# Hyena gate behind an RWKV-6 recurrence: a full inverse transform, sums from PSUM, interleaved products, and the key copy on VectorE

## The chip, the cores and the metric

The kernel runs on one core of one Trainium2 chip. The metric is the device time of one execution in microseconds (us), as the median of several runs. A "profiled span" is the length of the one execution that the profiler recorded; it is some 2 us shorter than the timed runs. Runs are marked fast or slow by their time (slow: over 1.5% above the fastest run of the same kernel); the comparisons of times below use the fast ones. The "granted clock" is the share of TensorE's full clock that the profiler shows it was given; 0.5 is half clock.

The program keeps its tiles in two memories: SBUF, and PSUM, to which it has TensorE write the results of all its matmuls and transposes.

## The reference, cut to what matters

Two stages stand one after the other. Stage 1 is a linear-attention recurrence over 768 steps for 4 batches and 8 heads of 48 columns. Stage 2 takes its output as `x` (4 x 768 x 384), projects it three ways, convolves one part with a filter through a real Fourier transform, gates it with the other two, and projects it out.

```python
# stage 1, per step t
cur = np.einsum('bhd,bhe->bhde', u[None] * kt, vt)
y[:, :, t] = np.einsum('bhd,bhde->bhe', rt, state + cur)
state = wt[:, :, :, None] * state + np.einsum('bhd,bhe->bhde', kt, vt)
# stage 2
x1, x2, x3 = split(x @ w_proj, 3)
X2 = np.fft.rfft(x2, n=S, axis=1)
H  = np.fft.rfft(filter_fft, n=S, axis=0)[None]
x2_conv = np.fft.irfft(X2 * H, n=S, axis=1)
return ((x1 * x2_conv * x3) @ w_out).astype(np.float32)
```

## The kernel before

Stage 1 works on chunks of 128 steps, six to a batch, 24 in all. One chunk is a serial loop across the engines:

- GpSimd scales the keys (`kh`), TensorE transposes them into PSUM (`tk`), and an engine copies them to SBUF (`tkT`).
- TensorE makes the scores (`sc`), VectorE masks them (`mt`), TensorE makes the output (`yn`), ScalarE copies it (`xn`), TensorE transposes it (`yt`), and ScalarE copies that into the tile `xT` for stage 2.

The start of `mt` is the clock by which I measure chunks: "chunk 9 at 81.0" means that its masked scores started 81.0 us into the span.

Stage 2 is cut into pieces that wait in a list, `pending`. Three calls of `fill` per chunk take pieces from it, by a budget of units. A unit is a group of matmuls plus its way out of PSUM. In the timelines of these runs VectorE and ScalarE run their operations in the order in which the program emits them, also where the first has to wait and the second could go (in chunk 0 of after the keys lie ready at 12.63, and the key copy on VectorE starts at 14.59, behind a bonus sum that waits 1.68 us for GpSimd; the key copy back on ScalarE, below, shows such a place too: ready at 81.46, started at 82.67). So the place of a call in the program is its place in its engine's queue.

```python
    def turn(idx):                       # start of a chunk
        tk = psA.tile([L, HP, L], BF16, tag="a", name="tk")
        ...                              # four transposes of kh
        nc.scalar.activation(out=tkT, in_=tk, func=AF.Copy)

    def turn_x(idx, xT):                 # end of a chunk
        yt = psA.tile([L, CB, L], BF16, tag="a", name="yt")
        ...                              # three transposes of xn
        nc.scalar.activation(out=xT[:, :, ci * L:(ci + 1) * L], in_=yt, func=AF.Copy)
    # ---- stage 2 of a batch (cut) ----
        def sums(ti):                    # once each for chunks 3, 4, 5 of a batch
            lo = xT[:, :, ti * L:(ti + 1) * L]
            hi = xT[:, :, HALF + ti * L:HALF + (ti + 1) * L]
            nc.vector.tensor_add(z("sd0")[:, :, sl], lo, hi)
            nc.vector.tensor_sub(z("sd1")[:, :, sl], lo, hi)

        def prods(sl):                   # six operations in a row, 128 x 1152 each
            nc.vector.tensor_mul(ua, xr, HR[:, sl, :])
            ...                          # mul, sub, mul, mul, add

        def inv(cb):                     # even and odd halves by symmetry, then combined
            ...                          # four full and four half-row matmuls -> ev, od
            nc.scalar.activation(out=ods, in_=od, func=AF.Copy)
            nc.vector.tensor_add(eo[:, 0, :], ev, ods)
            nc.vector.tensor_sub(eo[:, 1, :], ev, ods)
            nc.vector.tensor_mul(z("y")[:, cb, :], eo.rearrange("p q t -> p (q t)"), z("g")[:, cb, :])
        ...
            ready[5] += fws + [F(prods, slice(0, 3))]
            ready[5] += g1[0:4] + invs[0:1] + g1[4:6] + invs[1:3]
    # ---- the loop over chunks (cut) ----
    FILL = (2, 2, 2, 0)
            turn(idx); begin(idx + 2); load_weights(idx); issue_loads(idx + 4); fill(FILL[0])
            ...                          # late pieces join pending here
            scores(idx); decay(idx + 1); bonus_b(idx + 1); bonus_a(idx + 2); fill(FILL[1])
            output(idx); fill(FILL[2])
            turn_x(idx, xTs[b])
            ...                          # sums of this chunk, at once
                if idx == 3:
                    late = filters + late      # transform of the filter, six units
```

In the profile's names, `sd` are the sums, `X` the spectra, `U` and `P` the products, `g` the gate, `cc` the bonus sum of stage 1, `lw` the logarithm of the decay.

Of the kernel before, what the change touches and what calls it, by code (L numbers as in the profile page):

```python
# [10 lines left out]
FP32 = mybir.dt.float32  # L11
BF16 = mybir.dt.bfloat16
INT32 = mybir.dt.int32
AF = mybir.ActivationFunctionType
ALU = mybir.AluOpType
# [5 lines left out]
L = 128  # L21
NCH = S // L
C = H * D
CB = C // L
HP = H // 2
DP = 64
HALF = S // 2
NT = HALF // L
# [6 lines left out]
def kernel(  # L35
# [12 lines left out]
    nc = tc.nc  # L48
# [121 lines left out]
    nc.vector.memset(blk[DP:L, 1:2], 1.0)  # L170

    scl0 = consts.tile([L, 1], FP32)
    nc.vector.memset(scl0, 2.0 / S)
    nc.vector.memset(scl0[0:1, :], 1.0 / S)

# [8 lines left out]
    wout = consts.tile([L, CB, C], BF16)  # L184

    def load_weights(n):
        if n == 1:
            nc.sync.dma_start(
                out=filt, in_=moe_filter_fft.rearrange("(n p) c -> p n c", p=L)
            )  # L190
        elif n == -1:
            nc.gpsimd.dma_start(
                out=wproj, in_=moe_w_proj.rearrange("(n p) f -> p n f", p=L)
            )
        elif n == 2:
            nc.gpsimd.dma_start(
                out=wout, in_=moe_w_out.rearrange("(n p) f -> p n f", p=L)
            )

    m2 = consts.tile([L, 6, HALF], BF16)  # L200
    HR = consts.tile([L, 3, C], BF16)
    HI = consts.tile([L, 3, C], BF16)
    HG = consts.tile([L, 3, C], BF16)
# [2 lines left out]
    def ps2(name):  # L206
        return psA.tile([L, C], FP32, tag="a", name=name)
# [28 lines left out]
    sums = {}  # L236

    def setup_m2(q):
        tp = psA.tile([L, NT, L], BF16, tag="a", name="m2t")
        for ti in range(NT):  # L240
            nc.tensor.transpose(tp[:, ti, :], F[:, ti, q * L:(q + 1) * L], ident)
        nc.scalar.activation(out=m2[:, q, :], in_=tp.rearrange("p a b -> p (a b)"), func=AF.Copy)

    def setup_h(q):
        if not sums:
# [73 lines left out]
    def turn(idx):  # L319
        t = st[idx]  # L320
        kh = k_bufs[idx % NK]
        tk = psA.tile([L, HP, L], BF16, tag="a", name="tk")
        for j in range(HP):
            nc.tensor.transpose(tk[:, j, :], kh[:, 2 * j:2 * j + 2, :], ident)  # L324
        tkT = s1.tile([L, HP, L], BF16, tag="tkT", name="tkT")
        nc.scalar.activation(out=tkT, in_=tk, func=AF.Copy)  # L326
        t["tkT"] = tkT

    def scores(idx):
# [46 lines left out]
        nc.scalar.activation(out=xn, in_=y, func=AF.Copy)  # L376
        t["xn"] = xn

    def turn_x(idx, xT):
        b, ci = chunks[idx]  # L380
        t = st.pop(idx)
        yt = psA.tile([L, CB, L], BF16, tag="a", name="yt")
        for cb in range(CB):
            nc.tensor.transpose(yt[:, cb, :], t["xn"][:, cb * L:(cb + 1) * L], ident)  # L384
        nc.scalar.activation(
            out=xT[:, :, ci * L:(ci + 1) * L], in_=yt, func=AF.Copy
        )
        if ci < NCH - 1:
            st[idx + 1]["S"] = t["nxt"]
# [3 lines left out]
    stage2 = {}  # L393

    def make_stage2(b, xT):
# [3 lines left out]
            X0=([L, 3, C], BF16, 1), X1=([L, 3, C], BF16, 1),  # L399
            P0=([L, 3, C], BF16, 1), P1=([L, 3, C], BF16, 1),  # L400
            U0=([L, 3, C], BF16, 1), U1=([L, 3, C], BF16, 1),
            sd0=([L, CB, HALF], BF16, 1), sd1=([L, CB, HALF], BF16, 1),
        )
        made = {}

        def z(name):
            if name not in made:
                shape, dt, bufs = shapes[name]
                made[name] = s2.tile(shape, dt, tag=name, name=name, bufs=bufs)
            return made[name]  # L410
# [17 lines left out]
                z("g")[:, fb, sl], proj(2 * C + fb * L, sl), z("x1")[:, fb, sl]  # L428
            )

        def sums(ti):
            lo = xT[:, :, ti * L:(ti + 1) * L]
            hi = xT[:, :, HALF + ti * L:HALF + (ti + 1) * L]
            sl = slice(ti * L, (ti + 1) * L)
            nc.vector.tensor_add(z(f"sd{0}")[:, :, sl], lo, hi)
            nc.vector.tensor_sub(z(f"sd{1}")[:, :, sl], lo, hi)

        def x2(q, ti):
            ps = ps2("ps_x2")
# [8 lines left out]
            ps = fwd(q, z("ab")[:, 0], z("ab")[:, 1])  # L448
            nc.scalar.activation(out=z(f"X{q % 2}")[:, q // 2, :], in_=ps, func=AF.Copy)

        def prods(sl):
            xr, xi, pr, pi, ua, ub = (
                z(n)[:, sl, :] for n in ("X0", "X1", "P0", "P1", "U0", "U1")
            )
            nc.vector.tensor_mul(ua, xr, HR[:, sl, :])
            nc.vector.tensor_mul(ub, xi, HI[:, sl, :])
            nc.vector.tensor_sub(pr, ua, ub)
            nc.vector.tensor_mul(ua, xr, HI[:, sl, :])
            nc.vector.tensor_mul(ub, xi, HG[:, sl, :])
            nc.vector.tensor_add(pi, ua, ub)  # L460

        def inv(cb):
            col = slice(cb * L, (cb + 1) * L)
            ev, od = ps2("ps_e"), ps2("ps_o")
            full = ((0, 0, 0, ev), (1, 1, 0, ev), (4, 0, 2, od), (5, 1, 2, od))
            for n, (q, ri, sl, ps) in enumerate(full):
                nc.tensor.matmul(
                    ps, z(f"P{ri}")[:, sl, col], m2[:, q, :],
                    start=(n % 2 == 0), stop=False,
                )  # L470
            for ri in (0, 1):
                for q, ps in ((0, ev), (1, od)):
                    rows = slice(DP * q, DP * q + DP)
                    nc.tensor.matmul(  # L474
                        ps, z(f"P{ri}")[rows, 1, col], m2[rows, 2 + ri, :],
                        start=False, stop=(ri == 1),
                    )
            ods = s2.tile([L, HALF], FP32, tag="ods", name="ods", bufs=2)
            eo = s2.tile([L, 2, HALF], BF16, tag="eo", name="eo", bufs=2)
            nc.scalar.activation(out=ods, in_=od, func=AF.Copy)  # L480
            nc.vector.tensor_add(eo[:, 0, :], ev, ods)  # L481
            nc.vector.tensor_sub(eo[:, 1, :], ev, ods)  # L482
            nc.vector.tensor_mul(  # L483
                z("y")[:, cb, :], eo.rearrange("p q t -> p (q t)"), z("g")[:, cb, :]
            )

        def outp(ti):
            ps = ps2("ps_o")
# [11 lines left out]
        def F(f, *a):  # L500
            return (COST[f], lambda: f(*a))

        COST = {x1: 1, x3: 1, sums: 0, x2: 1, fw: 1, prods: 0, inv: 2, outp: 1}

        def gates(hf):
            return [F(f, fb, halves[hf]) for fb in range(CB) for f in (x1, x3)]

        ready = {2: gates(0)}
        for ti in range(NT):
            ready[NT + ti] = [F(sums, ti)] + [F(x2, q, ti) for q in (0, 1)]  # L510
        g1 = gates(1)
        fws = [F(fw, q) for q in range(6)]
        invs = [F(inv, cb) for cb in range(CB)]
        if b < B - 1:
            ready[5] += fws + [F(prods, slice(0, 3))]
            ready[5] += g1[0:4] + invs[0:1] + g1[4:6] + invs[1:3]
        else:
            ready[5][1:1] = g1[0:2]
            ready[5] += fws[0:2] + g1[2:3]
            ready[5] += [F(prods, slice(0, 1))] + fws[2:4] + g1[3:4]  # L520
            ready[5] += [F(prods, slice(1, 2))] + fws[4:6]
            ready[5] += [F(prods, slice(2, 3))] + g1[4:6] + invs
        ready[6] = [F(outp, ti) for ti in range(NCH)]
        return ready


# [10 lines left out]
        credit[0] = min(credit[0], 0)  # L537

    xTs = {}
    FILL = (2, 2, 2, 0)  # L540
    issue_loads(2)
    issue_loads(3)
    ENG = mybir.EngineType
    with tc.manual_schedule(engines={ENG.PE, ENG.Activation, ENG.DVE, ENG.Pool, ENG.SP}):
        begin(0)
        decay(0)
        bonus_a(0)
        begin(1)
        bonus_b(0)
        load_weights(-1)  # L550
        bonus_a(1)
        late, outs = [], []
        for idx in range(len(chunks)):
            b, ci = chunks[idx]
            if ci == 0:
                xTs[b] = s2.tile([L, CB, S], BF16, tag="xT", bufs=2, name=f"xT{b}")
            turn(idx)
            begin(idx + 2)
            load_weights(idx)
            issue_loads(idx + 4)  # L560
            fill(FILL[0])
            if late and ci == 3 and outs:
                pending.extend(late)
                pending.extend(outs)
                outs = []
            else:
                pending.extend(late)
            scores(idx)
            decay(idx + 1)
            bonus_b(idx + 1)  # L570
            bonus_a(idx + 2)
            fill(FILL[1])
            output(idx)
            fill(FILL[2])
            turn_x(idx, xTs[b])
            late = []
            if ci == 2:
                stage2[b] = make_stage2(b, xTs[b])
            if b in stage2:
                late = stage2[b].get(ci, [])  # L580
                if ci > 2:
                    late.pop(0)[1]()
                if idx == 3:
                    late = filters + late
                if ci == 5:
                    outs = stage2[b][6]
            fill(FILL[3])
        pending.extend(late + outs)
        fill(1000)
# [30 lines left out]
```

## Time and profile before

| | before |
|---|---|
| median time (runs) | 203.55 us (202.64 to 204.12) |
| profiled span, mean granted TensorE clock | 202.9 us, 0.932 |
| TensorE / VectorE / ScalarE busy | 77% / 76% / 62% |

From the page of before: busy time by engine, the granted TensorE clock in 40 slices of the span (9 is full), and the chain of waits by engine.

```profile
PE 156.5 (77%) x1490; PEld 97.7 (48%) x1490; DVE 153.6 (76%) x249; ACT 126.5 (62%) x269; POOL 121.6 (60%) x162
...
PEclk9999696996999969999999799999997999999678
...
DVE 31%; PE 25%; issue 12%; ACT 12%; DMA 8%; SPq 6%; POOL 4%; DVEq 0%; ACTq 0%; POOLq 0%
```

No engine is full on average. TensorE and VectorE are equally busy, and the chain changes engines all the time. This is a kernel whose regimes alternate, and the next view shows the two: windows of before, with stretch, length, then the busy us of TensorE, its weight loads, VectorE, ScalarE and GpSimd (number of instructions in brackets), granted clock, DMA share and GB/s.

```profile
65.00:73.00 8.00, 4.81 (x45) 2.84 (x43) 7.90 (x9) 3.67 (x8) 7.09 (x6) 0.98 0.56 103
73.00:81.00 8.00, 8.00 (x75) 4.54 (x73) 7.93 (x13) 4.45 (x10) 4.72 (x6) 0.81 0.55 96
...
98.00:103.00 5.00, 5.00 (x59) 3.36 (x57) 3.09 (x5) 4.97 (x13) 3.69 (x6) 1.00 1.18 242
```

In the first two stretches VectorE is full (7.90 and 7.93 of 8 us). In the third it has 2 us to spare and TensorE and ScalarE are full. The VectorE timeline shows what fills the first stretch: start, duration, engine, line, operation, output and inputs.

```profile
65.66 1.39 DVE L456 TENSOR_TENSOR U_1078<-X_962,HI 128x1152 bf16<-128x1152 bf16 x1
...
70.93 1.43 DVE L460 TENSOR_TENSOR P_1076<-U_1077,U_1078 128x1152 bf16<-128x1152 bf16 x1
...
73.22 1.21 DVE L343 TENSOR_TENSOR mt<-sc,mask_excl 128x1024 bf16<-128x1024 f32 x1
```

Six products stand in a row, over 7 us, with stage 1's mask behind them. From chunk 9 on the pattern repeats with a period of 40.8 us: chunk 9 starts at 81.0, chunk 15 at 121.8, chunk 21 at 162.7.

Three waits: engine and line waited for, us in total, times, longest.

```profile
ACT lw_82 L268 <- DMA ld_w<-in_w_dram: 5.2, 1, 5.2
...
PE ps_f L223 <- DVE fs L232: 3.7, 1, 3.7
...
PE ps_e L467 <- DVE P_1076 L460: 3.2, 1, 3.2
```

The first is the load of chunk 5, issued behind the 1152 KB filter load (at 26.8 and 26.1 us): it took 9.4 us from issue to landing, the median of such loads 4.0. The second is TensorE waiting for the sums of the filter. The third is TensorE waiting for the products, once per batch.

Last, the costs of the operations that the change touches, from the groups of instructions: busy us, mean ns of one, then idle time before it.

```profile
L326 ACT ACTIVATE tkT<-tk 128x512 bf16<-128x512 bf16 x24 | 14.4, 598 | 2.1 <-PE tk L324 2.1
...
L483 DVE TENSOR_TENSOR y<-eo,g 128x768 bf16<-128x768 bf16 x12 | 14.0, 1164 | 0.4
```

And the same for the sums, with shapes kept apart:

```profile
L436 DVE TENSOR_TENSOR sd_1353<-xT_866 128x384 bf16<-128x384 bf16 x3 | 2.9, 962 | 0.0
```

`y` takes 1.28 to 1.41 us while GpSimd works and 0.56 us in the tail where it does not. The sums behave alike: 0.35 us at best, 1.16 us at worst. Both read two SBUF inputs.

### The profile page before, as it was taken

The numbers are of one execution on the slowest core, as the hardware profiler recorded it, in microseconds if no ns is written. First come the engines' busy times: TensorE is split into PE (matmuls) and PEld (weight loads), VectorE is DVE, ScalarE is ACT, GpSimd is POOL, SyncE is SP. The second block draws the span as 40 slices with busy tenths as digits, with TensorE's granted clock in tenths as the row PEclk, the third lists the DMA queues.
The fourth block names the chain that finished last, engine by engine and source line by source line (L and its number), as shares of the span: only waits on it lengthen the run. The fifth ranks groups of instructions, "written<-read, shape, count | busy, mean of one in ns | idle before, by whom it ended". The sixth has DMA issues, their size and how long they took to land.

```text
span 202.9 us, 4168 instructions
## 1 busy us (share of the span) xinstructions
PE 156.5 (77%) x1490; PEld 97.7 (48%) x1490; DVE 153.6 (76%) x249; ACT 126.5 (62%) x269; POOL 121.6 (60%) x162
## 2 busy tenths in 40 slices
PE   0177768629989679779996697799976977996962
PEld 0055645416666436546664365466642554653230
DVE  8344553598687999997869999978699999459730
ACT  3866461825989517659996166599961654983242
POOL 5089895577479929459789394597893845100000
PEclk9999696996999969999999799999997999999678
DMA  6999989799987871833989928339930000140024
GB/s 132 198 196 186 207 229 247 152 179 218 189 156 136 156 129 26 155 72 81 288 149 207 176 48 155 60 76 296 168 68 0 5 0 0 57 179 2 0 78 155
DMA packets 104804, 26.41 MB, mean 130 GB/s; under 512 B 100048, under 2 KB 104400, under 8 KB 104784
## 3 DMA queue, kind: packets, MB, share of 16 engines
q1 hardware_dynamic: 103984, 24.98, 60.7%
q0 software_dynamic: 800, 1.18, 3.4%
q8 instruction: 11, 0.18, 0.4%
q14 instruction: 9, 0.07, 0.1%
HBM read 22.61 MB, written 4.72 MB: 135 GB/s over the span
## 4 chain that ended last, share of the span: by engine, by line
DVE 31%; PE 25%; issue 12%; ACT 12%; DMA 8%; SPq 6%; POOL 4%; DVEq 0%; ACTq 0%; POOLq 0%
DMA ld_w<-in_w_dram 8%; DVE mt L343 6%; PE ps_p L415 4%; PE ps_o L490 4%; DVE g L427 4%; ACT tkT L326 3%; PE yn L371 2%; DVE cc L290 2%; SPq L91 2%; ACT ab L445 2%; PE sc L338 2%; DVE eo L481 2%; DVE eo L482 2%; DVE qT L316 2%; ACT o L494 2%
## 5 line engine op out<-in xcount | busy, mean ns | idle before, releaser
L291 POOL TENSOR_TENSOR vc<-v,cc 128x384 bf16<-128x384 bf16 x24 | 21.9, 912 | 34.6 <-PE yt L384 16.5
L343 DVE TENSOR_TENSOR mt<-sc,mask_excl 128x1024 bf16<-128x1024 f32 x24 | 29.2, 1215 | 12.4 <-PE sc L338 12.4
L281 POOL TENSOR_TENSOR rku<-rk,u_bc 128x384 bf16<-128x384 bf16 x24 | 24.4, 1019 | 1.9
L376 ACT ACTIVATE xn<-yn 128x384 bf16<-128x384 f32 x24 | 11.8, 490 | 14.5 <-PE yn L371 13.8
L312 POOL TENSOR_TENSOR kh_83<-ld_k,en 128x384 bf16<-128x384 f32 x12 | 12.0, 1000 | 14.4 <-ACT en L310 14.2
L480 ACT ACTIVATE ods<-ps_o 128x384 f32<-128x384 f32 x12 | 5.9, 490 | 22.8 <-PE ps_o L474 20.6
L415 PEld LDWEIGHTS <-wproj 128*128 128x128 bf16 x144 | 13.9, 104 | 9.1 <-issue 3.5
L310 ACT ACTIVATE en<-csi 128x384 f32<-128x384 f32 x24 | 11.9, 497 | 8.7 <-PE csi L301 7.4
L490 PE MATMUL ps_o<-wout,y 128*128 128x384 bf16 x72 | 15.4, 356 | 1.7 <-DVE y L483 1.6
L326 ACT ACTIVATE tkT<-tk 128x512 bf16<-128x512 bf16 x24 | 14.4, 598 | 2.1 <-PE tk L324 2.1
L316 DVE TENSOR_TENSOR qT<-rT,e_85 128x512 bf16<-128x512 f32 x12 | 8.2, 687 | 9.8 <-PE rT L307 5.3
L290 DVE TENSOR_REDUCE cc<-rku 128x8 f32<-128x384 bf16 x24 | 13.0, 541 | 2.9 <-POOL rku L281 2.9
L282 POOL CAST v<-ld_v 128x384 bf16<-128x384 f32 x24 | 14.4, 602 | 0.0
L483 DVE TENSOR_TENSOR y<-eo,g 128x768 bf16<-128x768 bf16 x12 | 14.0, 1164 | 0.4
L494 ACT ACTIVATE o<-ps_o 128x384 f32<-128x384 f32 x24 | 11.5, 498 | 4.1 <-PE ps_o L490 4.1
L312 POOL TENSOR_TENSOR kh_84<-ld_k,en 128x384 bf16<-128x384 f32 x12 | 13.8, 1148 | 0.2
L371 PE MATMUL yn<-v,mt 128*128 128x48 bf16 x192 | 9.7, 192 | 5.1 <-DVE mt L343 5.1
L338 PE MATMUL sc<-qT,tkT 48*128 48x128 bf16 x192 | 9.7, 222 | 3.8 <-ACT tkT L326 3.3
L301 PE MATMUL csi<-lw_81,mask_incl 128*128 128x384 bf16 x12 | 4.5, 374 | 9.6 <-ACT lw_81 L268 9.6
L363 PE MATMUL yn<-vc,ident 128*128 128x384 bf16 x24 | 9.0, 376 | 3.2 <-ACT en L310 1.8
L371 PEld LDWEIGHTS <-mt 128*128 128x128 bf16 x192 | 7.9, 103 | 6.8 <-DVE mt L343 6.3
L338 PEld LDWEIGHTS <-tkT 48*128 48x128 bf16 x192 | 5.7, 95 | 10.8 <-ACT tkT L326 10.3
(279 smaller groups left out, 482.1 us busy)
## 6 DMA issues: line engine op xcount, KB each, us to landing
ld_w<-in_w_dram SPq DMA_DIRECT2D x24, 192.0 KB, 3.9
ld_k<-in_k_dram SPq DMA_DIRECT2D x24, 192.0 KB, 3.8
ld_v<-in_v_dram SPq DMA_DIRECT2D x24, 192.0 KB, 4.0
out_dram<-o SPq DMA_DIRECT2D x3, 1152.0 KB, 5.1
filt<-in_moe_filter_fft_dram SPq DMA_DIRECT2D x1, 1152.0 KB, 7.8
out_dram<-o SPq DMA_DIRECT2D x6, 192.0 KB, 1.9
r_76<-in_r_dram SPq DMA_DIRECT2D x5, 192.0 KB, 3.6
r_77<-in_r_dram SPq DMA_DIRECT2D x5, 192.0 KB, 4.5
```

What stands on the lines that cost most here:

```text
L281: nc.gpsimd.tensor_mul(t["rku"], rk, u_bc)
L282: nc.gpsimd.tensor_copy(out=t["vb"], in_=t["lv"])
L290: nc.vector.tensor_reduce(out=cc, in_=t["rku"], axis=AX.X, op=ALU.add)
L291: nc.gpsimd.tensor_mul(t["vc"], t["vb"], cc.to_broadcast([L, H, D]))
L312: nc.gpsimd.tensor_mul(kh[:, :, 0:D], t["lk"], en)
L326: nc.scalar.activation(out=tkT, in_=tk, func=AF.Copy)
L338: nc.tensor.matmul(sc[:, par, j, :], tkT[p0:p0 + D, j, :], qT[p0:p0 + D, j, :], start=True, stop=True,)
L343: nc.vector.tensor_mul(mt, sc.rearrange("p q j t -> p (q j) t"), _mid(mask_excl, H))
L371: nc.tensor.matmul(y[:, h, :], mt[:, HP * (h % 2) + h // 2, :], vb[:, h, :], start=False, stop=(h == H - 1),)
L415: nc.tensor.matmul(ps, wproj[:, cb, col0:col0 + L], xT[:, cb, sl], start=(cb == 0), stop=(cb == CB - 1),)
L490: nc.tensor.matmul(ps, z("y")[:, cb, ti * L:(ti + 1) * L], wout[:, cb, :], start=(cb == 0), stop=(cb == CB - 1),)
L494: nc.scalar.activation(out=z("o")[:, ti, :], in_=ps, func=AF.Copy)
```

## The change

Its intent is to take work off VectorE and ScalarE and give it to TensorE.

- **Inverse.** It computes all 768 rows with matmuls (twelve per column block, with negated copies `m2n` of the transform). There is nothing to copy out and combine: `y` is one multiply per half, straight from PSUM.
- **Sums.** They read the fresh half from the PSUM tile `yt` instead of from SBUF, and are emitted before ScalarE's copy of that tile.
- **Products.** They are six pieces with matmul pieces between them.
- **Key copy.** It moves from ScalarE to VectorE.
- **Start.** The filter load and the load of the output weights are issued one chunk later, the projection weights behind `bonus_a(1)`, and the filter's transform goes into the products' batch of pieces, two chunks later.
- **Budget.** It rises from 6 to 7 units per chunk.

```diff
@@ load_weights
-        if n == 1:                     # filter
+        if n == 2:
-        elif n == 2:                   # output weights
+        elif n == 3:
@@ setup_m2 (cut)
+        if q in (2, 3):                # and q >= 4, with scalar1=-1.0
+            nc.vector.tensor_scalar(out=m2n[:, q - 2, :], in0=m2[:, q, :], scalar1=sgn, ...)
@@ turn
-        nc.scalar.activation(out=tkT, in_=tk, func=AF.Copy)
+        nc.vector.tensor_copy(out=tkT, in_=tk)
@@ turn_x
+        if ci >= NT:
+            sums(ci - NT, yt)
         nc.scalar.activation(
             out=xT[:, :, ci * L:(ci + 1) * L], in_=yt, func=AF.Copy
         )
@@ sums
-            hi = xT[:, :, HALF + ti * L:HALF + (ti + 1) * L]     # hi is now the PSUM tile
@@ inv (the whole even/odd version removed)
+        def inv(cb, hf):
+            ps = ps2("ps_i")
+            for q in range(6):
+                m = m2n[:, q - 2, :] if (hf and q >= 2) else m2[:, q, :]
+                nc.tensor.matmul(ps, z(f"P{q % 2}")[:, q // 2, cb * L:(cb + 1) * L], m,
+                                 start=(q == 0), stop=(q == 5))
+            nc.vector.tensor_mul(z("y")[:, cb, sl], ps, z("g")[:, cb, sl])
@@ order of the pieces
+            ready[5] += [f[0], f[2], f[4], p[0], g[0], g[1], p[1], f[1], f[3], f[5], p[2]]
+            ready[5] += [g[2], p[3], g[3], p[4], g[4], p[5], g[5]] + lo + hi
@@ main loop (cut)
-    FILL = (2, 2, 2, 0)
+    FILL = (2, 2, 2, 1)
-        load_weights(-1)
         bonus_a(1)
+        load_weights(-1)
-                if idx == 3:
-                    late = filters + late
+                    if b == 0:         # at chunk 5
+                        late = late[:5] + filters + late[5:]
```

## The prediction

> **What bounds the kernel now.** 203 us, 24 chunks, four batches of six. The chain of waits: VectorE 31%, TensorE 25%, issue 12%, ScalarE 12%, DMA 8%. By stage:
>
> - Start-up (0 to 31 us): DMA-bound. In the ScalarE timeline the logarithm of chunk 5 waits 5.2 us for its load, behind the 1152 KB filter load.
> - Filter transform: in the VectorE timeline the masked scores of chunk 4 start at 41.6, those of chunk 5 at 52.2 us (others without stage-2 load: about 5).
> - Then a period of 40.8 us per batch (the products start at 65.0, 105.8, 146.8). Two regimes: VectorE saturated about 26 us (six products alone 7.2 us, the chunk around them 10.9 us, next two 7.7 and 7.1), while TensorE waits 3.2 us for the products and its granted clock falls to 0.77-0.89; then about 15 us in which TensorE and ScalarE are both 4.9 of 5 us busy and VectorE about 3 (table of windows), chunks of 4.7 to 5.4 us.
> - Tail: 28.7 us from the last masked scores to the end.
>
> **What the change does, per batch**, in start-to-start intervals of the trace.
> VectorE: loses six even/odd combines (0.47 each, -2.8); y becomes six half multiplies from PSUM (0.47 each) instead of three from SBUF (about 1.3 while GpSimd works, -1.0); sums read PSUM, so only one SBUF input (six at about 0.47 instead of about 4.0 in all, -1.2). [...] the same y takes 1.34 us with GpSimd busy, 0.56 in the tail without. It gains six key copies; none is in this trace. [...] Net about -2.6: 36 -> 33 us.
> ScalarE: loses six key copies (0.60) and three odd copies (0.49): -5 us busy.
> TensorE: each inverse column block becomes twelve matmuls, 1.96 us, from 0.98 (the half-row pairs overlapped): +2.9 us per batch. Work units per chunk rise from 6 to 7, and it becomes the fullest engine: 2.35 + 7 x 0.486 = 5.75 us per chunk.
>
> **Critical path.** The ScalarE saving is mostly off it. The products are spread over three chunks with gates between, so VectorE intervals per chunk become about 3, 5.4, 9.7, 5.4, 5.4, 4.4 us. Taking the larger of TensorE and VectorE chunk by chunk: 5 x 5.75 + 9.7 = 38.5 us per batch, 2.3 less than now.
> Start: the filter load now follows chunk 5's load, so the 5.2 us wait nearly goes; the filter transform moves from chunk 5 to chunk 7, where it costs about 4 us extra rather than 5.5. Masked scores of chunk 9 move from 81.0 to about 72: the largest gain, -9 us.
> Two periods: -4.7 us. Tail: the deferred filter work leaves about six units of backlog, and the last inverse has 18 more matmul slots, less the removed ScalarE copy and combines: +2 us. Sum -11.7, plus 1.5 us for new stalls.
>
> **Predicted: 193.0 us, 80% range 187.5 to 198.5.** Faster by over 2%: 0.90; within 2%: 0.09; slower: 0.01.
>
> **Right if:** key copy 0.35-0.5 us on VectorE; sums and y about 0.55 us each; no wait of 5 us on the load of chunk 5; products 37.5-39.5 us apart; TensorE busy share above 80%, granted clock above 0.94; one long chunk (9 to 10 us) per batch; a tail of 30 us or more.
> **Wrong if:** the key copy, in order behind products and sums, holds the scores back in every chunk (periods of 40 us or more); PSUM reads of the same tile by both engines slow each other; the load wait only moves to chunk 6 or 7; the tail's matmuls run long at the throttled clock.

The other was a term of the VectorE sum. That sum came to -2.6 us per batch (36 to 33), as it still says, while the three terms that remain come to -5.0: the fourth was my figure for the six key copies that VectorE gains. In before no such copy is on VectorE; in after they take 0.418 us each, +2.5 us per batch. The intervals per chunk, and the range for the key copy under "Right if", rest on the same figure, for which no trace then stood. In the 38.5 us of a period it is one copy, in the chunk of 9.7. The 0.47 us for `y` and for the sums are an estimate too: the start-to-start interval of the combines in before (75.87 and 76.33, for example), which read one operand from PSUM.

## The result

| | before | after |
|---|---|---|
| median time (runs) | 203.55 us (202.64 to 204.12) | 195.36 us (194.59 to 197.55) |
| profiled span, mean granted clock | 202.9 us, 0.932 | 193.0 us, 0.973 |
| TensorE / VectorE / ScalarE busy | 77% / 76% / 62% | 82% / 73% / 57% |

The ratio of the times is 0.959 (95% interval 0.952 to 0.965). Ratios here are the mean time of one kernel's fast runs over that of the other's fast runs of the same rounds, so they are not quite the ratio of the medians in the table.

From the page of after, the lines that answer to those of before:

```profile
PE 157.3 (82%) x1538; PEld 103.8 (54%) x1538; DVE 140.8 (73%) x267; ACT 110.0 (57%) x233; POOL 117.5 (61%) x162
...
PEclk9999958999999999999999969999999999999999
...
PE 66%; DVE 18%; issue 6%; ACT 5%; DMA 2%; POOL 2%; SPq 0%; ACTq 0%; DVEq 0%; POOLq 0%
```

The chain has become a TensorE chain: 66%, from 25%. ScalarE lost 16.5 us and VectorE 12.8 us of work, and TensorE is now what bounds the steady part. The windows of after, same columns:

```profile
65.00:74.10 9.10, 6.57 (x67) 3.83 (x65) 8.46 (x14) 4.27 (x9) 6.51 (x7) 1.00 0.99 155
...
91.10:96.80 5.70, 5.70 (x59) 3.85 (x60) 3.27 (x6) 5.70 (x15) 4.32 (x7) 1.00 0.54 159
```

One chunk per batch, the one with the last products, is still VectorE's: 8.46 of 9.1 us. An ordinary chunk holds seven units. The one in the second window takes 5.60 us (from 91.14 to 96.75; the window is 0.1 us wider), and TensorE is busy in all of it. The VectorE timeline of the same kind of stretch, one batch later:

```profile
106.96 1.27 DVE L477 TENSOR_TENSOR P_1800<-U_1802,U_1803 128x1152 bf16<-128x1152 bf16 x1
108.15 0.55 DVE L442 TENSOR_TENSOR g<-ps_p,x_1440 128x384 bf16<-128x384 f32 x1
...
109.62 0.41 DVE L338 COPY tkT<-tk 128x512 bf16<-128x512 bf16 x1
109.95 1.13 DVE L481 TENSOR_TENSOR P_1801<-U_1804,U_1805 128x1152 bf16<-128x1152 bf16 x1
```

Products are spread, and the key copy stands among them and not behind all six. The waits of after:

```profile
ACT xT_2292 L399 <- DVE sd_2772 L450: 3.6, 3, 1.6
...
PE ps_i L487 <- DVE P_1801 L481: 2.5, 1, 2.5
...
PE ps_f L227 <- DVE fs L236: 2.5, 1, 2.5
```

The wait for chunk 5's load is gone. The wait for products is 2.5 us per batch, from 3.2. The first line is new, and the view has one such for each of the four batches: ScalarE's copy of `yt` waits 13.5 us in all for VectorE's sums, which read the same tile and are emitted first. This is a wait of the program, and what the trace shows is the price of the order.

And the costs, by groups of VectorE instructions with shapes kept apart:

```profile
L492 DVE TENSOR_TENSOR y<-ps_i,g 128x384 bf16<-128x384 f32 x24 | 13.3, 556 | 8.6 <-PE ps_i L487 8.6
...
L338 DVE COPY tkT<-tk 128x512 bf16<-128x512 bf16 x24 | 10.0, 418 | 6.8 <-PE tk L336 6.6
...
L450 DVE TENSOR_TENSOR sd_1326<-xT_829,yt 128x384 bf16<-128x384 bf16 x3 | 1.0, 347 | 0.0
```

**Where the 9.9 us of the two profiles lie**, by the start of the masked scores (each figure rounded by itself):

| stretch | before | after | gain |
|---|---|---|---|
| to chunk 4 | 41.6 | 39.6 | 1.9 |
| chunk 4 to 5 (filter work before) | 10.7 | 4.6 | 6.1 |
| chunk 5 to 7 (filter work after) | 10.0 | 14.1 | -4.1 |
| chunk 7 to 9 (products of batch 0) | 18.7 | 15.8 | 2.9 |
| chunk 9 to 15, first period | 40.8 | 38.6 | 2.3 |
| chunk 15 to 21, second period | 40.9 | 40.2 | 0.7 |
| chunk 21 to 23 | 11.6 | 11.8 | -0.3 |
| from chunk 23 to the end | 28.6 | 28.3 | 0.3 |

The second period after is 1.7 us longer than the first, though it has the same work. The trace says why: after the wait for the products TensorE ran for about 3.4 us at half clock. A window of after:

```profile
112.60:116.00 3.40, 3.40 (x20) 2.32 (x19) 2.88 (x5) 1.01 (x2) 1.16 (x2) 0.51 0.00 0
```

The granted clock was 0.51, and the chunk took 7.19 us where the same chunk of the first period took 5.52. In the stretch the inverse's matmuls start every 0.32 us, after it every 0.16. The same 2.5 us wait stands in all three batches, and in this profile only here was it followed by half clock. That is not the chance of one run: eight profiles of this document keep the order of products that makes this wait, and half clock followed it in seven of them in the second batch, in three in the first and in three in the third.

The traces also show what goes with it. In each profile the half-clock stretches begin whole multiples of 3.41 us apart (in before at 72.7, 113.6 and 154.6, twelve times 3.41 from one to the next). Cut into windows of that grid, the window just before the stretch at 112.7 had no matmul in 1.9 of its 3.41 us. The emptiest windows at the two other waits had none in 1.7 and 1.4 us and were not followed by half clock: there the edge of the grid split the wait. Over the 14 profiles, from 18 us on, 60 windows at full clock were followed by half clock, and 56 of them were idle for at least half of their length; of the 594 others 4 were. (In before and after alone: 9 of 10, and 1 of 80.) (The ends of matmuls are modelled, so windows near one half can fall on either side.) No run was made to test this. How much of the scatter between runs (194 to 199 us, at a mean clock of 0.98 to 0.95) comes from such stretches is open, since no more than two runs of a kernel were traced.

### The profile page after: what moved, and what is told of

Its sections match the earlier page's. It is cut to its first block, busy times and chain, and to the rows that moved or that the text cites. A ratio compares the mean times of both kernels' runs of the same rounds, so it can differ in the third digit from the quotient of the medians.

```text
span 193.0 us, 4267 instructions
## 1 busy us (share of the span) xinstructions
PE 157.3 (82%) x1538; PEld 103.8 (54%) x1538; DVE 140.8 (73%) x267; ACT 110.0 (57%) x233; POOL 117.5 (61%) x162
## 4 chain that ended last, share of the span: by engine, by line
PE 66%; DVE 18%; issue 6%; ACT 5%; DMA 2%; POOL 2%; SPq 0%; ACTq 0%; DVEq 0%; POOLq 0%
PE ps_i L487 11%; PE ps_p L430 7%; PE rT L319 6%; PE ps_o L497 5%; PE sc L350 5%; PE ps_f L227 4%; PE csT L315 3%; PE yn L383 3%; PE ps_f L219 2%; DVE tkT L338 2%; PE csi L313 2%; PE kv L360 2%; PE kv L362 2%; PE yn L375 2%; PE yt L396 2%
## 5 line engine op out<-in xcount | busy, mean ns | idle before, releaser
L303 POOL TENSOR_TENSOR vc<-v,cc 128x384 bf16<-128x384 bf16 x24 | 21.0, 874 | 15.9 <-DVE cc L302 8.7
L324 POOL TENSOR_TENSOR kh_83<-ld_k,en 128x384 bf16<-128x384 f32 x12 | 12.0, 1002 | 20.6 <-ACT en L322 20.6
L492 DVE TENSOR_TENSOR y<-ps_i,g 128x384 bf16<-128x384 f32 x24 | 13.3, 556 | 8.6 <-PE ps_i L487 8.6
L388 ACT ACTIVATE xn<-yn 128x384 bf16<-128x384 f32 x24 | 11.8, 491 | 12.7 <-PE yn L383 11.7
L294 POOL CAST v<-ld_v 128x384 bf16<-128x384 f32 x24 | 16.6, 692 | 0.0
L430 PEld LDWEIGHTS <-wproj 128*128 128x128 bf16 x144 | 12.5, 97 | 5.6 <-issue 0.3
L324 POOL TENSOR_TENSOR kh_84<-ld_k,en 128x384 bf16<-128x384 f32 x12 | 12.0, 1004 | 5.5 <-ACT en L322 5.4
L338 DVE COPY tkT<-tk 128x512 bf16<-128x512 bf16 x24 | 10.0, 418 | 6.8 <-PE tk L336 6.6
L497 PE MATMUL ps_o<-wout,y 128*128 128x384 bf16 x72 | 13.8, 326 | 0.0
L367 DVE TENSOR_TENSOR S<-kv,phi 128x384 bf16<-128x384 f32 x20 | 10.9, 546 | 0.0
L396 PE MATMUL yt<-ident,xn 128*128 128x128 bf16 x72 | 8.3, 227 | 2.5 <-ACT xn L388 2.5
L227 PE MATMUL ps_f<-ab,F 128*128 128x384 bf16 x48 | 10.1, 327 | 0.0
```

What stands on the lines that cost most here:

```text
L227: nc.tensor.matmul(ps, F[:, ti, c0:c0 + L], x[:, ti, :], start=(ti == 0), stop=(ti == NT - 1),)
L294: nc.gpsimd.tensor_copy(out=t["vb"], in_=t["lv"])
L303: nc.gpsimd.tensor_mul(t["vc"], t["vb"], cc.to_broadcast([L, H, D]))
L324: nc.gpsimd.tensor_mul(kh[:, :, 0:D], t["lk"], en)
L338: nc.vector.tensor_copy(out=tkT, in_=tk)
L430: nc.tensor.matmul(ps, wproj[:, cb, col0:col0 + L], xT[:, cb, sl], start=(cb == 0), stop=(cb == CB - 1),)
```

## The experiments

Twelve runs, all results correct against the reference. Each ratio is against runs of the kernel before on the same chip, with 5 rounds. The first call ran on one chip and the other two on another, where the changed kernel itself was not repeated. "Undo" edits start from the changed kernel; its own repeat is the first run.

### The changed kernel again

No edit. 

> Control: the changed kernel once more, on the chip of the next three runs. Both theories: 0.955 to 0.965 of the kernel before. It gives the base against which the others are read.

Measured: 196.42 us, ratio 0.961 (0.954 to 0.968), profiled span 193.0. The result repeats. Undo edits are compared with this ratio below.

### The load order alone, on the kernel before

```diff
-        if n == 1:            # filter
+        if n == 2:
-        elif n == 2:          # output weights
+        elif n == 3:
-        load_weights(-1)
         bonus_a(1)
+        load_weights(-1)
```

> The kernel before with nothing changed but the order of the weight loads (filter load one chunk later, after the load of chunk 5; output weights one chunk later; projection weights after the products of chunk 1). Theory A (the filter load in front of the load of chunk 5 costs about 5 us, and that time is really saved): the 5.2 us wait of the logarithm of chunk 5 goes, masked scores of chunk 5 start near 48 instead of 52.2 us, whole kernel 4 us faster: ratio 0.975 to 0.985. Theory B (the loads are the bound up to about 50 us, so the wait only moves to a later chunk): ratio 0.995 to 1.005.

Measured: 202.6 us, ratio 0.998 (0.992 to 1.004), so the same. The profile is of a slow run, but at the clock of the profile of before (0.932). The load wait shrank from 5.2 us to 1.0, and chunk 4 came at 38.7 in place of 41.6. Then chunk 4 to 5 took 11.7 us in place of 10.7, and by chunk 9 the lead was down to 1.1 us. VectorE timeline and one wait of this run:

```profile
40.85 0.54 DVE L290 TENSOR_REDUCE cc<-rku 128x8 f32<-128x384 bf16 x1
41.31 1.35 DVE L232 TENSOR_TENSOR fs<-filt 128x1152 bf16<-128x1152 f32 x1
```

```profile
PE ps_f L223 <- DVE fs L232: 4.6, 1, 4.6
```

The filter sums start only behind the mask and the rest of the chunk's VectorE work, and TensorE waits 4.6 us for them (3.7 before). The wait on the load gave part of its time to the next fixed stage. Taking away a visible wait of 5 us was, by itself, worth nothing that can be told from zero.

### The old load order, in the changed kernel

```diff
-        if n == 2:            # filter
+        if n == 1:
-        elif n == 3:          # output weights
+        elif n == 2:
-        bonus_a(1)
         load_weights(-1)
+        bonus_a(1)
```

> The changed kernel with the load order of before. Theory A: a wait of about 4 to 5 us on the load of chunk 5 comes back and the kernel is 3 to 5 us slower than the control (0.975 to 0.985 of before). Theory B: within 1 us of the control.

Measured: 197.56 us, ratio 0.969 (0.962 to 0.976): 0.8% more than the changed kernel, and the intervals overlap. Its only profile fell in a slow run with half-clock stretches (mean clock 0.948), so I read no more from it than that chunk 4 came 3.0 us later. By the ratios the loads are worth about 1.6 us of the 8. That lies between the two theories and can't be told from zero.

### The key copy back on ScalarE

```diff
-        nc.vector.tensor_copy(out=tkT, in_=tk)
+        nc.scalar.activation(out=tkT, in_=tk, func=AF.Copy)
```

> The changed kernel with the transposed keys copied out of PSUM by ScalarE again (0.60 us each instead of 0.42 on VectorE). Theory A (the move is a load balance for the TensorE-bound chunks, but costs at the start, where the copy stands behind the bonus sum and the four negated-matrix multiplies on VectorE): masked scores of chunk 0 start near 14.3 again and of chunk 1 near 21.5, the long product chunk gets 0.4 us shorter, the TensorE-bound chunks stay at 5.3 to 5.8; total 0 to 2 us faster than the control. Theory B (taking 0.6 us per chunk off ScalarE is what makes the chunks short): chunks with seven units lengthen by 0.3 to 0.6 us, 24 chunks, total 4 to 8 us slower than the control.

Measured: 202.19 us, ratio 0.993 (0.985 to 1.000). The profile is of a slow run; the fast runs took 200.5 to 202.2 us. It costs 3.3% (0.9925 / 0.9611), and my own theory, that ScalarE has room for it, fell. The other theory had the size right and the place wrong: chunks with seven units and no sums did not move (5.65 us against 5.60). The chunks with sums did: chunks 10 and 11, at a granted clock of 1.00, took 6.78 and 6.15 us against 6.31 and 5.24. ScalarE timeline of this run; the bracket is idle time before it, and who ended it:

```profile
82.28 0.49 ACT L399 ACTIVATE xT<-yt 128x384 bf16<-128x384 bf16 x1 [1.60 <-DVE sd L450]
82.67 0.59 ACT L338 ACTIVATE tkT<-tk 128x512 bf16<-128x512 bf16 x1
```

The transposes into `yt` had ended at 81.24. ScalarE's copy starts at 82.28, because it comes after VectorE's sums, so 1.04 of its 1.60 idle us are due to the order. The keys lay ready in PSUM at 81.46, and the key copy starts at 82.67: it stands behind that copy in ScalarE's queue. The scores wait for the key copy: TensorE waits for `tkT` 13 times here, 12.0 us in all. ScalarE is only 59% busy. It is not short of time; its queue is held up at the wrong place.

### Key copy on ScalarE, and ScalarE first at the shared tile

If that is the cause, letting ScalarE read `yt` before VectorE's sums should cure it with the key copy still on ScalarE.

```diff
-        nc.vector.tensor_copy(out=tkT, in_=tk)
+        nc.scalar.activation(out=tkT, in_=tk, func=AF.Copy)
@@ turn_x
-        if ci >= NT:
-            sums(ci - NT, yt)
         nc.scalar.activation(out=xT[...], in_=yt, func=AF.Copy)
+        if ci >= NT:
+            sums(ci - NT, yt)
```

> The changed kernel with the keys copied by ScalarE (as in the run that was 5 us slower), and the ScalarE copy of the transposed tile put in program order before the VectorE sums that read the same PSUM tile: the reader that comes second waits for the first, so now ScalarE does not wait. Theory A (the loss came from ScalarE's order: its tile copy waits up to 1.6 us for VectorE's sums and the key copy stands behind it, so the scores come late): the waits of the tile copy on the sums go, the chunks with sums return to within 0.3 us of those of the changed kernel, the total is within 2 us of it. Theory B (the 0.6 us of ScalarE work per chunk is itself what is lost): the kernel stays 4 to 6 us slower than the changed kernel, near 0.99 of before.

Measured: 193.57 us, ratio 0.951 (0.945 to 0.958). It is cured. The ratio is 1% below that of the change (0.961), but the intervals overlap. The same place in the ScalarE timeline:

```profile
82.82 0.49 ACT L397 ACTIVATE xT<-yt 128x384 bf16<-128x384 bf16 x1 [0.59 <-PE yt L396]
...
83.70 0.59 ACT L338 ACTIVATE tkT<-tk 128x512 bf16<-128x512 bf16 x1
```

The copy now waits only for its own transpose. TensorE's wait for `tkT` fell from 12.0 to 3.7 us, and now the sums wait for the copy (5.5 us in all), which does not show in the time.

### Key copy on VectorE, and ScalarE first

The fourth corner of that square. It was run at another time.

```diff
@@ turn_x of the changed kernel
-        if ci >= NT:
-            sums(ci - NT, yt)
         nc.scalar.activation(out=xT[...], in_=yt, func=AF.Copy)
+        if ci >= NT:
+            sums(ci - NT, yt)
```

> The changed kernel with only the order of the two readers of the transposed tile turned round: ScalarE's copy first, VectorE's sums (still from PSUM) second; the keys stay on VectorE. It splits the 15 us that sums from SBUF cost. Theory A (waiting 0.5 us for ScalarE in front of the key copy on VectorE is most of it): the sums start 0.5 us later, the chunks with sums lengthen by 0.3 to 1 us as they did there, total 4 to 12 us slower than the changed kernel. Theory B (the long contended sums, 0.4 and 1.1 us, are it): sums stay at 0.35 us, the key copy comes less than 0.5 us later, which the slack of about 0.4 us in front of the scores swallows, total within 2 us of the changed kernel.

Measured: 201.61 us, ratio 0.986 (0.980 to 0.993). Neither theory held as a whole. Its profile is 6.9 us longer than that of the changed kernel. In the two periods the swap costs little, 0.4 and 0.3 us. Chunks 4 to 7 cost 4.0 us, and two half-clock stretches lie there (from 45.5 and from 52.3 us), where the changed kernel has none. A half-clock stretch at 158.1 adds 1.9 us: 7.40 us for a chunk of 5.52. Another 1.2 us were lost by chunk 2, before the first sums, where the edit has no part. VectorE timeline of this run:

```profile
51.48 0.35 DVE L449 TENSOR_TENSOR sd<-xT,yt 128x384 bf16<-128x384 bf16 x1 [2.36 <-ACT xT L397]
...
52.02 0.42 DVE L338 COPY tkT<-tk 128x512 bf16<-128x512 bf16 x1
```

It is the key copy on ScalarE mirrored, but the delay is smaller. The transposes into `yt` had ended at 50.92 and the sums start at 51.48, behind ScalarE's copy, so 0.56 of the 2.36 us are due to the order; the rest is waiting that any order has. The key copy stands behind the sums. The four corners:

| | VectorE reads `yt` first | ScalarE reads `yt` first |
|---|---|---|
| key copy on VectorE | 0.959, 0.961 (the change) | 0.986 |
| key copy on ScalarE | 0.993 | **0.951** |

A direct measure of the delay is the time from the end of the transposes into `yt` (as the trace models it) to the end of the key copy. In chunks 9 to 11 it is 1.2 to 1.3 us in the changed kernel, 1.5 to 1.7 with ScalarE first, 2.0 to 2.4 with the key copy on ScalarE, and 1.0 to 1.6 in the best corner. So with the key copy on ScalarE the order is worth 0.5 to 1.0 us a chunk, and the fast runs had the clock of the changed kernel (0.97): there the cause is shown. With the key copy on VectorE the order is worth 0.2 to 0.6 us a chunk, and most of the 5 us goes with half clock (24.7 us of it in this profile, 10.2 in that of the changed kernel); whether the later key copies brought on all of those stretches is not shown.

Of the four, the better two have the key copy on the engine that goes first at the shared tile. Asking only which engine has more free time (ScalarE, in both columns) gives the wrong answer in the left one. With the key copy's engine second, the kernel took 2.6% longer with the key copy on VectorE (0.986 against 0.961, half clock included) and 4.3% longer with it on ScalarE (0.993 against 0.951).

### The sums from SBUF again

```diff
@@ turn_x of the changed kernel
-        if ci >= NT:
-            sums(ci - NT, yt)
         nc.scalar.activation(out=xT[...], in_=yt, func=AF.Copy)
+        if ci >= NT:
+            sums(ci - NT, xT[:, :, ci * L:(ci + 1) * L])
```

> The changed kernel with the sums taken from SBUF after ScalarE's copy, as before. Theory A (sums from PSUM are worth something only because the key copy now stands behind them on VectorE): the sums start 0.5 us later and take 0.4 and 1.1 us instead of 0.35 and 0.35, the key copy and the scores come 0.5 to 1 us late in each chunk with sums, three a batch, and the kernel is 3 to 7 us slower than the changed one. Theory B (the sums lie in chunks that TensorE bounds, so their length does not matter): within 1 us.

Measured: 212.18 us, ratio 1.031 (1.020 to 1.042, two fast runs only). This is far more than expected. Timelines of VectorE and, last line, GpSimd in this run:

```profile
89.34 0.36 DVE L449 TENSOR_TENSOR sd<-xT 128x384 bf16<-128x384 bf16 x1
89.61 1.07 DVE L450 TENSOR_TENSOR sd<-xT 128x384 bf16<-128x384 bf16 x1
90.61 0.41 DVE L338 COPY tkT<-tk 128x512 bf16<-128x512 bf16 x1
...
89.41 1.06 POOL L293 TENSOR_TENSOR rku<-rk,u_bc 128x384 bf16<-128x384 bf16 x1
```

Two effects add up. The sums must wait for ScalarE's copy, and one of them takes 1.07 us in place of 0.35 while GpSimd's `rku` runs beside it. The key copy stands behind both: it ends 2.2 to 2.5 us after the transposes into `yt` in chunks 9 to 11, and TensorE waits for it 14 times, 17.2 us. The profile is of a slow run, but chunks 10 and 11, at a granted clock of 1.00, take 6.81 and 6.50 us where the changed kernel has 6.31 and 5.24. Chunk 9, partly at half clock, takes 7.73 for 5.52. The largest part, 6.8 us, lies in chunks 4 to 7, with half clock in each of them, so the two effects are not all of the loss. `y` of before, which also reads two SBUF inputs, shows the same: 1.28 to 1.41 us while GpSimd works, 0.56 in the tail. With one input in PSUM the sums of after take 0.35 us beside GpSimd too (at 89.39, beside `rk`).

### The products in a row again

```diff
-            ready[5] += [f[0], f[2], f[4], p[0], g[0], g[1], p[1], f[1], f[3], f[5], p[2]]
-            ready[5] += [g[2], p[3], g[3], p[4], g[4], p[5], g[5]] + lo + hi
+            ready[5] += [f[0], f[2], f[4], f[1], f[3], f[5]] + p + g + lo + hi
```

> The changed kernel with the six products issued in one row after the six transforms instead of spread between gates and inverse. Theory A: one chunk a batch rises from 9.1 to about 11 us, TensorE idles 3 us or more in it, total 3 to 6 us slower than the changed kernel. Theory B (VectorE has the same work either way): within 1 us.

Measured: 203.14 us, ratio 1.000 (0.993 to 1.006). The whole gain of the change is gone. The product chunk takes 11.65 to 11.83 us (9.1 in the changed kernel), and the waits for products grow to:

```profile
PE ps_i L487 <- DVE P L477: 8.7, 4, 2.6
...
PE ps_i L487 <- DVE P L481: 4.5, 4, 1.4
```

That is 13.2 us in four batches, from 8.6 in the changed kernel, and the kernel takes about 7 us longer, for an order of pieces that adds no work. The waits are 4.6 us of that; half clock rose from 10.2 to 23.9 us in the profile, 3.4 of that before chunk 3, where this edit has no part.

### The even/odd inverse again

Before's `inv`, six units per chunk, everything else of the change kept. This is not before's own arrangement, since the combines now share VectorE with the key copy.

```diff
-    FILL = (2, 2, 2, 1)
+    FILL = (2, 2, 2, 0)
@@ inv as in the kernel before; the order of the pieces
-  + lo + hi
+  + invs
```

> The changed kernel with the inverse of before (even and odd parts, ScalarE copy, two combines and a 768-wide multiply on VectorE; six units a chunk instead of seven). Theory A: the chunks with inverses become bound by VectorE again (7 to 9 us for the chunk with two or three of them), the TensorE-bound ones fall to about 5.2; together 1 us a period more, total 1 to 4 us slower than the changed kernel. Theory B (the full inverse only costs TensorE time, and the spread products and the moved keys make all of the gain): 1 to 3 us faster.

Measured: 211.25 us, ratio 1.040 (1.034 to 1.046), also far more than expected. Its waits, and a place in its VectorE timeline:

```profile
ACT xT L399 <- DVE sd L450: 20.5, 10, 3.5
...
PE sc L350 <- DVE tkT L338: 15.0, 14, 2.5
...
79.53 0.56 DVE L502 TENSOR_TENSOR eo<-ps_e,ods 128x384 bf16<-128x384 f32 x1 [1.24 <-ACT ods L501]
...
81.59 0.42 DVE L338 COPY tkT<-tk 128x512 bf16<-128x512 bf16 x1
```

The two queues now hold each other up in both directions. VectorE's combines wait for ScalarE's `ods` (8.6 us in all), ScalarE's `xT` waits for VectorE's sums, and `ods` or the sums can stand behind either. The key copy comes behind all of it: in chunks 9 and 10 it ends 2.6 and 3.6 us after the transposes into `yt`, in the changed kernel 1.3, and chunk 9 takes 12.05 us for 5.52. So the full inverse takes off more than busy time: it also removes an exchange between VectorE and ScalarE. The budget of six units came with this edit and was not tested alone.

### Better versions

From the best corner (key copy on ScalarE, ScalarE first), three more. First, the filter transform goes where the list of pieces is short (after chunk 3's pieces):

```diff
-                    if b == 0:
-                        late = late[:5] + filters + late[5:]
+                if idx == NT:
+                    late = late + filters
```

> The fastest so far (keys on ScalarE, copy first, 193.6 us) with the filter transform three chunks earlier, in the chunks that have fewer units than slots. Theory A (the changed kernel carries six units of backlog from the late filter transform to the tail, where each costs 0.49 us): the tail from the last masked scores to the end falls from 28.4 to about 25.5 us, total 2 to 4 us faster. Theory B (the filter chunk costs VectorE and TensorE the same wherever it stands, and early it meets the loads): within 1.5 us.

Measured: 188.39 us, ratio 0.922 (0.916 to 0.929), profiled span 186.9. The change put six units of filter work in front of the first batch's products. As every chunk is full from then on, those six units were never caught up and stood in the tail. Here the tail from chunk 23 is 25.4 us (28.3 in the corner without this edit), as expected, and both periods are 38.0 us (38.4 and 40.0 in the corner, whose second one has a half-clock stretch worth 1.7). Up to chunk 9 this version is 0.7 us behind the corner. With the pieces shifted in this way the waits for the last products are 1.1 us at most, where the corner had 2.5, and half clock appears in no period. So some 2 of the 5 us gained are not the backlog that I had named. The granted clock of this run in 40 slices:

```profile
PEclk9999999996999999999999999999999999999999
```

Second, the negated transform `m2n` written by ScalarE in pieces of its own, to clear VectorE's queue at chunk 1 (the filter place unchanged):

```diff
-            nc.vector.tensor_scalar(out=m2n[:, q - 2, :], in0=m2[:, q, :], ...)   # both branches
+    def setup_m2n(q):
+        nc.scalar.activation(out=m2n[:, q - 2, :], in_=m2[:, q, :], func=AF.Copy,
+                             scale=sgn if q < 4 else -1.0)
+    pending += [(2, lambda q=q: setup_m2n(q)) for q in range(2, 6)]
```

> The fastest so far with the four negated inverse matrices written by ScalarE from SBUF, one every two units in chunks 1 and 2, instead of by VectorE in chunk 0. Theory A (on VectorE they hold the masked scores of chunk 1 back, from 20.8 to 22.0 us, and this delay is kept to the end): masked scores of chunk 1 near 21.0, total 0.5 to 1.5 us faster. Theory B (the loads of chunks 2 to 6 are the bound up to there and swallow it): masked scores of chunk 6 and the total unchanged within 0.5 us.

Measured: 192.59 us, ratio 0.946 (0.939 to 0.953). Against the corner's 0.951 the intervals overlap, so it is inconclusive. Chunk 1 came at 21.8, hardly before the corner's 22.0: there it waits for GpSimd's keys.

Third, both edits.

> Both of the two runs before this one together. If both theories A hold: 2.5 to 5 us faster than the fastest so far, about 189 to 191 us, 0.93 to 0.94 of before. If neither: 193 to 194 us, 0.95.

Measured: 188.35 us, ratio 0.924 (0.918 to 0.928): nothing over the filter edit alone. The version with the filter edit is the one to keep; it is 7.8% below the kernel before.

## Why the prediction was right or wrong

The total was right: 193.0 predicted, 195.36 measured, in the range. So were most of the signs:

- **Key copy on VectorE**: 0.418 us (0.410 to 0.426; 0.35 to 0.5 predicted).
- **`y` halves**: 0.556 us (about 0.55 predicted). They take 0.546 to 0.559 us while GpSimd works and in the tail alike, where `y` of before, twice as wide, took 1.28 to 1.41 us while GpSimd worked and 0.56 in the tail.
- **Load wait**: the 5.2 us for chunk 5 is gone; 1.3 us on chunk 2's load is what is left.
- **TensorE the fullest engine**: 82% busy, clock 0.973 (above 80% and 0.94 predicted). Taking the larger of TensorE and VectorE chunk by chunk gave 38.5 us for the period, and the first was 38.6. Two errors cancel in that: the five ordinary chunks took 5.24 to 6.78 us, 5.89 on average (5.75 predicted), and the long one 9.1 (9.7 in the sum).
- **Long chunk**: one per batch, 9.1 us (9 to 10 predicted).

Wrong in size were these terms of the sum:

- **"Sums about 0.55 us each"**: they took 0.35. I had put any operation with a PSUM input at one length, an estimate. It fits the combines of before (0.54 to 0.56) and `y` of after (0.556), which read fp32 from PSUM. The sums read bf16 from PSUM and bf16 from SBUF; they take 0.347 us, like the shortest sums of before with both inputs in SBUF (0.35). The term is 12 x 0.2 us on VectorE over the two middle periods, where TensorE bounds most chunks, so it hardly showed in the time.
- **"Masked scores of chunk 9 move from 81.0 to about 72: the largest gain, -9 us"**: it was 6.9. I had looked at the waits that go and not at what the start gains in VectorE work. Chunks 0 to 3 came 1.1 to 1.7 us later than before, 1.7 at chunk 3, which is most of the 2.1 us missing. The timeline of after shows why:

```profile
14.12 0.55 DVE L302 TENSOR_REDUCE cc<-rku 128x8 f32<-128x384 bf16 x1 [1.68 <-POOL rku L293]
14.59 0.41 DVE L338 COPY tkT<-tk 128x512 bf16<-128x512 bf16 x1
...
20.11 2.02 DVE L252 TENSOR_SCALAR m2n<-m_174 128x384 bf16<-128x384 bf16 x2
22.05 0.41 DVE L338 COPY tkT<-tk 128x512 bf16<-128x512 bf16 x1
```

  In chunk 0 the key copy stands behind a bonus sum that waits for GpSimd, in chunk 1 behind four multiplies that make `m2n` (3.2 us). With the key copy back on ScalarE, chunks 0 and 1 came 1.1 and 0.9 us earlier.

- **"Two periods: -4.7 us"**: they gave 2.9. The first gave 2.3 as predicted, the second 0.7 because of the half-clock stretch after the wait for the products; at 40.2 us it lies outside the 37.5 to 39.5 that I had asked for. For the kernel before I had put the lower clock beside the wait for the products. In the sum for the changed kernel I left it out, though a wait stays there.
- **"Tail: +2 us" and "a tail of 30 us or more"**: it was 28.3, 0.3 shorter than before. The backlog was there, as the filter edit shows: moving it took 3.0 us off the tail of the corner, near my six units. I left out that before's tail ran partly throttled: its clock was 0.76 from 190 us on, where after's was 1.00 over the whole tail. Before's tail has 7.3 us at half clock, which can cost up to half of that, 3.6 us. That the better clock paid for the extra work is my estimate from these figures; no run tests it.
- **"Plus 1.5 us for new stalls"** was an allowance for misses of this kind and has no measured counterpart of its own.

The errors of the start (+2.1), the periods (+1.8), the two chunks before the tail (+0.3), the tail (-2.3) and the stall allowance (-1.5) sum to about +0.3 us in the profiled span. That the total came out is partly luck.

Two steps of the reasoning were weaker than the sum shows, and only the experiments told:

- **The largest gain at the start, named together with the loads.** The load order alone is worth 0.2% on the kernel before and some 0.8% in the changed one. The 6.1 us between chunks 4 and 5 come from moving the filter's transform out of there (put back there by the filter edit, this interval is 10.6 us again), and 4.1 of them are paid back between 5 and 7.
- **"The ScalarE saving is mostly off the critical path."** True of ScalarE's load: with the order at the shared tile right, the copies back on ScalarE cost nothing (0.951 against 0.961, intervals overlapping). Not true of its queue: with the order left as it is, they cost 3.3%. I had listed "PSUM reads of the same tile by both engines slow each other" as a danger. The program keeps the two reads apart, and each took as long in both orders (the sums 0.35 us, ScalarE's copy 0.49); it is the wait for one another that moves, and which queue it stops.

The parts are not additive. Undoing one alone costs, by ratio to the changed kernel, 0.8% (loads), 3.3% (key copy), 4.0% (products), 7.3% (sums) and 8.2% (inverse): 24% together, for a change worth 4%. What the waits show is that three of them meet in one place: with the key copy, the sums or the inverse undone, TensorE waits 12.0, 17.2 and 15.0 us for `tkT`, where the changed kernel has 7.1 (these three profiles: one fast run, two slow). The products meet elsewhere, in TensorE's wait for them. The kernel before, with the same sums and inverse at 203 us, escapes it: its key copy is on ScalarE, and its sums, which read SBUF, come after ScalarE's copy, so it is on the good side of the square. In its trace the key copy ends 1.0 to 1.2 us after the transposes, as in the best corner.

One part of these costs is not separated: the clock. The profiles of the kernels with the products, the sums or the inverse undone, or with the order swapped, have 22 to 25 us at half clock, the changed kernel's has 10.2. At most half of the difference, about 6 to 7.6 us, is time lost to it, by my estimate (the 3.4 us at half clock in the second period of after cost 1.7). It goes with longer waits, by the count of windows above, but no run takes it away.

## What to carry to other kernels

Before moving an operation to the engine with more free time, list what stands in front of it in that engine's queue and whether any of it waits for another engine; where two engines read one PSUM tile, put the critical operation on the engine that reads first (cleanly shown here for ScalarE, less so for VectorE). Spread a row of long operations among the matmuls that don't need them, and put deferred work where the list of work is short, for a backlog in front of a full engine is carried to the end. Test a change of many parts by undoing them one at a time, and don't expect the parts to add up.
